# The last output tiles of a fused attention and gated-FFN kernel: column parts in PSUM tiles of their own, a narrow last part, and products left in PSUM

## The chip, the cores and the metric

One core of one Trainium2 chip. The metric is device time in microseconds (us) of one execution, lower is better. Every result is the median of several executions; all runs were fast (granted clock 0.998 to 1.000).

The engines are called by their names, with the profile's short forms: TensorE (PE; its weight loads PEld), VectorE (DVE), ScalarE (ACT), GpSimd (POOL), SyncE (SP). A "q" after a name is the engine's sequencer or queue. PSUM is the on-chip buffer that TensorE's results go to in this kernel, in tiles of 2 x 512 fp32 columns, of which each 512 are called a bank here; SBUF is the one that this kernel keeps the rest of its tiles in. A DMA's landing is its end in the profile.

## The reference, cut to what matters

```python
x  = A_x                                  # 1 x 2048 x 640
xn = layernorm(x)
s  = attention(xn)                        # 32 heads of 192, last 512 keys; ends in  o @ wo  (6144 x 640)
g  = silu(ffn(xn))                        # gated FFN
return x + s * g
```

The kernel treats the heads as 16 pairs and the 2048 rows as 4 blocks of 4 tiles of 128. Only the end is in question: for the last pair, each tile of 128 rows gets `o @ wo` for 640 columns (in PSUM), is multiplied by `g` (the tile `g2`), has the rest added (`sacc`, which already holds `x` and the other pairs' part times `g`), and is stored.

## The kernel before

The output tiles of the last pair. Tiles of block 2 and 3 take two groups of three matmuls per half, since they also take up the pair before.

```python
def wo_mm(ps, i, qt, n, first=True, end=True):
    for j in range(3):
        nc.tensor.matmul(ps, OTs[i][:, 3*qt+j, :], pairs[i//NB]["wo"][:, j, n*HD:(n+1)*HD], ...)   # HD = 320

def wo_last(b, qt, eng):
    i, t = last * NB + b, 4 * b + qt
    ob  = xrs[t] if b < 2 else finp.tile([P, D], bf, name="ob", bufs=4)
    s_f = finp.tile([P, 2, HD], f32, name="s_f", bufs=4)
    split = b == NB - 1 and qt == 3                       # the very last tile
    sc = None if split else mm_tile() if b >= 2 and qt % 2 == 0 else sc_tile()
    ps = [(mm_tile()[:, 0, :] if split else sc[:, n, :])[:, 0:HD] for n in range(2)]
    for n, cols in enumerate(halves):
        # ... matmuls of half n into ps[n]
        if split:
            nc.vector.tensor_tensor(s_f[:, n, :], ps[n], g2[:, t, cols], ALU.mult)
            nc.vector.tensor_tensor(ob[:, cols], s_f[:, n, :], sacc[:, t, cols], ALU.add)
            (nc.scalar if n else nc.sync).dma_start(...)
    if split:
        return
    nc.vector.tensor_tensor(s_f[:], sc[:, :, 0:HD], g2[:, t, :]..., ALU.mult)
    eng.tensor_tensor(ob[:], s_f[:]..., sacc[:, t, :], ALU.add)
    stores.append((t, ob))

# ... at the end
for b in (2, 3):
    for qt in range(4):
        store(0 if (b, qt) == (3, 3) else 3)
        wo_last(b, qt, V if b == 3 and qt % 2 == 0 else G)     # V = VectorE, G = GpSimd
```

`mm_tile()` and `sc_tile()` each hand out one of two PSUM tiles of two banks in turn: four tiles, eight banks. A product is always VectorE's (GpSimd reads only SBUF in this kernel), and the addition is GpSimd's, except for two tiles of block 3 and the last tile.

The softmax here doesn't subtract the row's maximum and nothing guards it: scores larger than these inputs give would overflow.

Of the kernel before, what the change touches and what calls it, by code (L numbers as in the profile page):

```python
# [10 lines left out]
ALU = mybir.AluOpType  # L11
# [4 lines left out]
def kernel(  # L16
# [13 lines left out]
    nc = tc.nc  # L30
    P = nc.NUM_PARTITIONS

    x2 = A_x.flatten_outer_dims()
    out2 = out.flatten_outer_dims()
    Sq, D = x2.shape
# [9 lines left out]
    NB = Sq // 512  # L45
# [5 lines left out]
    HD = D // 2  # L51
    scale = float(Dh) ** -0.5
    EPS = 1e-5
    bf = dt.bfloat16
    f32 = dt.float32
# [6 lines left out]
    kk, vv, wq, wo = A_k_cache[0], A_v_cache[0], A_wq, A_wo  # L62
# [8 lines left out]
    def sc_tile():  # L71
        return psum.tile([P, 2, 512], f32, name="sc", tag="sc")

    def mm_tile():
        return psum.tile([P, 2, 512], f32, name="mm", tag="mm")
# [5 lines left out]
    g2 = res.tile([P, T, D], bf, name="g2")  # L81
# [14 lines left out]
    pairs = {}  # L96
# [68 lines left out]
    with ExitStack() as fctx:  # L165
# [154 lines left out]
        first = {f: [sc[:, s, :] for s in range(2)] for f, sc in ((0, sc_tile()), (1, sc_tile()))}  # L320
# [89 lines left out]
    finp = ctx.enter_context(tc.tile_pool(name="fin", bufs=2))  # L410
    sacc = sapool.tile([P, T, D], f32, name="sacc")

    NS = NPAIR * NB
    turn_t = smpool.tile([P, 1], f32, name="turn_t", bufs=1)
    last = NPAIR - 1
    Ps, OTs, Obs, xrs = {}, {}, {}, {}
# [91 lines left out]
    def pv_full(i, q2):  # L508

        pr, b = divmod(i, NB)  # L510
        if q2 == 0:
            Obs[i] = opool.tile([P, 4, 2, Dh], bf, name="O_b")
            tag = "OT_l" if late(i) and pr < last else "OT_b"
            OTs[i] = otpool.tile([P, 12, P], bf, name=tag, tag=tag, bufs=2 if tag == "OT_l" else 3)
        O_b, OT_b = Obs[i], OTs[i]
        alone = i < 2 or (pr == last and 2 * b + q2 < 5)
        acc = sc_tile() if alone and b == 1 else mm_tile()
        for k in range(2):
            qt = 2 * q2 + k
            for h in range(2):  # L520
                for kc in range(KC):
                    nc.tensor.matmul(  # L522
                        acc[:, k, h * 256 : h * 256 + Dh + 1],
                        Ps[i][kc][:, h, qt * P : (qt + 1) * P], V_p[:, kc, h, 0 : Dh + 1],
                        start=(kc == 0), stop=(kc == KC - 1),
                    )
        divide(i, q2, acc, alone)
# [6 lines left out]
    def late(i):  # L534
        return i // NB >= NPAIR - 2 and i % NB >= 2

    def wo_mm(ps, i, qt, n, first=True, end=True):
        for j in range(3):
            nc.tensor.matmul(  # L539
                ps, OTs[i][:, 3 * qt + j, :], pairs[i // NB]["wo"][:, j, n * HD : (n + 1) * HD],  # L540
                start=(first and j == 0), stop=(end and j == 2),
            )

    def follows(m, earlier):
        tc.add_manual_dep(
            m.ins, earlier.ins.name,
            mybir.DependencyInfo(mybir.DependencyClass.Sync, mybir.DependencyReason.DATA),
            reason="row tiles change banks",
        )
# [48 lines left out]
    def wo_full(i, qt):  # L598
        pr, b = divmod(i, NB)
        t = 4 * b + qt  # L600
        sc = sc_tile()
        for n in range(2):
            wo_mm(sc[:, n, 0:HD], i, qt, n)
        s_t = sacc[:, t, :].rearrange("p (n d) -> p n d", n=2)
        if pr == 0:
            nc.vector.tensor_copy(out=s_t, in_=sc[:, :, 0:HD])
        else:
            nc.vector.tensor_tensor(s_t, s_t, sc[:, :, 0:HD], ALU.add)

        if pr == last - 1 or late(i + NB):  # L610
            nc.gpsimd.tensor_tensor(sacc[:, t, :], sacc[:, t, :], g2[:, t, :], ALU.mult)
            if pr < last - 1:
                add_x(t)

    def add_x(t):
        nc.gpsimd.tensor_tensor(sacc[:, t, :], sacc[:, t, :], xrs[t][:], ALU.add)

    stores = []

    def wo_last(b, qt, eng):  # L620
        i, t = last * NB + b, 4 * b + qt
        ob = xrs[t] if b < 2 else finp.tile([P, D], bf, name="ob", bufs=4)
        s_f = finp.tile([P, 2, HD], f32, name="s_f", bufs=4)
        halves = [slice(n * HD, (n + 1) * HD) for n in range(2)]
        split = b == NB - 1 and qt == 3
        sc = None if split else mm_tile() if b >= 2 and qt % 2 == 0 else sc_tile()
        ps = [(mm_tile()[:, 0, :] if split else sc[:, n, :])[:, 0:HD] for n in range(2)]
        for n, cols in enumerate(halves):
            if late(i):
                wo_mm(ps[n], i - NB, qt, n, end=False)  # L630
            wo_mm(ps[n], i, qt, n, first=not late(i))
            if split:
                nc.vector.tensor_tensor(s_f[:, n, :], ps[n], g2[:, t, cols], ALU.mult)
                nc.vector.tensor_tensor(ob[:, cols], s_f[:, n, :], sacc[:, t, cols], ALU.add)
                (nc.scalar if n else nc.sync).dma_start(
                    out=out2[t * P : (t + 1) * P, cols], in_=ob[:, cols]
                )
        if split:
            return
        nc.vector.tensor_tensor(  # L640
            s_f[:], sc[:, :, 0:HD], g2[:, t, :].rearrange("p (n d) -> p n d", n=2), ALU.mult
        )
        eng.tensor_tensor(ob[:], s_f[:].rearrange("p n d -> p (n d)"), sacc[:, t, :], ALU.add)
        stores.append((t, ob))

    def store(left):
        while len(stores) > left:
            t, ob = stores.pop(0)
            nc.sync.dma_start(out=out2[t * P : (t + 1) * P, :], in_=ob[:])
# [20 lines left out]
    for pr in range(NPAIR):  # L670
        for b in range(NB):
            i = pr * NB + b
# [22 lines left out]
        for b in range(NB):  # L695
            i = pr * NB + b
            if i < 2:
                two(pv(i, 0), pv(i, 1))
                if i == 0:
                    q_rows(*EARLY)  # L700
            elif pr < last - 1:
                woven(i)
            else:
                for q2 in range(2):
                    pv_full(i, q2)
                    wo_full(i - 2, 2 * q2)
                    wo_full(i - 2, 2 * q2 + 1)
            if b == 0 and pr + 2 < NPAIR:
                load_k(pr + 2)
            elif b == 1 and pr + 2 < NPAIR:  # L710
                load_wq(pr + 2)
            elif b == 2:
                load_wo(pr + 1)
    i = last * NB
    V, G = nc.vector, nc.gpsimd
# [3 lines left out]
    for b, q2, more in ((0, 0, (2, 1)), (0, 1, (3, 0)), (1, 0, (3, 1)), (1, 1, None)):  # L719
        for k in range(2):  # L720
            wo_last(b, 2 * q2 + k, G)
        if more:
            pv_full(i + more[0], more[1])
    for b in (2, 3):
        for qt in range(4):
            store(0 if (b, qt) == (3, 3) else 3)
            wo_last(b, qt, V if b == 3 and qt % 2 == 0 else G)


# [28 lines left out]
```

## Time and profile before

| | before |
|---|---|
| median of the first 3 runs | 925.28 us (924.81 to 925.31) |
| profiled span | 923.7 us |
| TensorE busy | 917.0 us |
| first matmul of block 2 of the last pair (the start of the "tail" in what follows) | 905.48 us |
| last issue of a store | 920.95 us, 15.47 after the tail's start |
| end of the span | 18.2 us after the tail's start |

How to read it: TensorE is busy from one end to the other (917.0 of 923.7 us), so almost all of the time is out of reach of this change. The prediction below shows the lines of the profile.

### The profile page before, as it was taken

The numbers are of one execution on the slowest core, as the hardware profiler recorded it, in microseconds if no ns is written. First come the engines' busy times: TensorE is split into PE (matmuls) and PEld (weight loads), VectorE is DVE, ScalarE is ACT, GpSimd is POOL, SyncE is SP. The second block draws the span as 40 slices with busy tenths as digits, with TensorE's granted clock in tenths as the row PEclk, the third lists the DMA queues.
The fourth block names the chain that finished last, engine by engine and source line by source line (L and its number), as shares of the span: only waits on it lengthen the run. The fifth ranks groups of instructions, "written<-read, shape, count | busy, mean of one in ns | idle before, by whom it ended". The sixth has DMA issues, their size and how long they took to land.

```text
span 923.7 us, 25785 instructions
## 1 busy us (share of the span) xinstructions
PE 917.0 (99%) x11101; PEld 626.2 (68%) x11101; DVE 576.2 (62%) x844; ACT 473.7 (51%) x847; POOL 100.1 (11%) x387
## 2 busy tenths in 40 slices
PE   9999999999999999999999999999999999999997
PEld 5455555575858585868686867676767777776665
DVE  6433331467676767676666667676767676767655
ACT  4222223546464656555556565655555555556561
POOL 0000000000000000000000000000000000002977
PEclk9999999999999999999999999999999999999999
DMA  9321510035544434444536252636271717162524
GB/s 294 77 53 35 114 35 1 1 71 95 83 82 83 83 79 87 74 91 68 98 59 106 60 107 53 112 51 115 44 121 41 126 37 129 36 132 74 135 57 140
DMA packets 243810, 77.18 MB, mean 84 GB/s; under 512 B 224624, under 2 KB 243696, under 8 KB 243696
## 3 DMA queue, kind: packets, MB, share of 16 engines
q1 hardware_dynamic: 242640, 74.72, 41.5%
q8 instruction: 87, 1.43, 0.7%
q10 hardware_dynamic: 1056, 0.82, 0.3%
q14 instruction: 27, 0.22, 0.1%
HBM read 39.45 MB, written 2.62 MB: 46 GB/s over the span
## 4 chain that ended last, share of the span: by engine, by line
PE 98%; DMA 1%; DVE 0%; ACTq 0%; issue 0%; DVEq 0%
PE mm L430 22%; PE sc L565 19%; PE sc L444 18%; PE mm L470 16%; PE sc L276 11%; PE mm L298 6%; PE sc L539 3%; PE mm L522 2%; PE mm L539 1%; DMA wu_sb<-in_B_w_up_dram 1%; PE mm L276 0%; PE mm L311 0%; PE sc L522 0%; PE sc L470 0%; PE mm L444 0%
## 5 line engine op out<-in xcount | busy, mean ns | idle before, releaser
L448 ACT ACTIVATE p_t<-sc 128x1024 bf16<-128x1024 f32 x254 | 252.9, 1022 | 128.6 <-PE sc L444 128.6
L435 DVE TENSOR_REDUCE qT<-mm 128x512 bf16<-128x1024 f32 x189 | 231.0, 1223 | 92.5 <-PE mm L430 90.0
L500 ACT ACTIVATE O_b<-mm,r 128x192 bf16<-128x192 f32 x486 | 164.6, 421 | 183.4 <-issue 159.2
L430 PE MATMUL mm<-xnT,wq_p 64*128 64x512 bf16 x1890 | 240.2, 377 | 0.0
L590 DVE TENSOR_TENSOR sacc<-sacc,sc 128x640 f32<-128x640 f32 x200 | 164.3, 821 | 89.5 <-PE sc L565 89.5
L565 PE MATMUL sc<-wo_p,OT_b 64*128 64x320 bf16 x2592 | 217.4, 296 | 0.0
L444 PE MATMUL sc<-qT,khat 64*128 64x512 bf16 x1524 | 198.4, 377 | 0.1
L470 PE MATMUL mm<-V_p,p_t 64*128 64x193 bf16 x3520 | 186.5, 243 | 0.0
L470 PEld LDWEIGHTS <-p_t 64*128 64x128 bf16 x3584 | 162.9, 93 | 12.3 <-issue 0.4
L430 PEld LDWEIGHTS <-wq_p 64*128 64x128 bf16 x1890 | 105.7, 94 | 94.5 <-issue 0.5
L565 PEld LDWEIGHTS <-OT_b 64*128 64x128 bf16 x2592 | 140.7, 94 | 21.1
L444 PEld LDWEIGHTS <-khat 64*128 64x128 bf16 x1536 | 85.9, 94 | 79.0 <-issue 0.4
L553 POOL MEMSET turn_t<- 128x1 f32 x328 | 32.2, 98 | 696.4 <-PE mm L470 474.0
L284 DVE TENSOR_TENSOR hT<-sc,sg 128x512 bf16<-128x512 f32 x46 | 31.7, 690 | 85.2 <-ACT sg L283 85.1
L283 ACT ACTIVATE sg<-sc 128x512 bf16<-128x512 f32 x46 | 27.3, 596 | 72.4 <-PE sc L276 72.4
L276 PE MATMUL sc<-xnT,wu_sb 128*128 128x512 bf16 (+1 forms) x260 | 59.1, 355 | 0.5 <-DMA wu_sb<-in_B_w_up_dram 0.5
L276 PE MATMUL sc<-xnT,wg_sb 128*128 128x512 bf16 (+1 forms) x260 | 59.2, 355 | 0.0
L298 PE MATMUL mm<-wd_sb,hT 128*128 128x320 bf16 x384 | 56.6, 300 | 0.0
L489 DVE RECIPROCAL r<-mm 128x4 f32<-128x4 f32 x124 | 22.6, 183 | 47.4 <-PE mm L470 35.9
L298 PEld LDWEIGHTS <-hT 128*128 128x128 bf16 x384 | 37.5, 98 | 18.9
L276 PEld LDWEIGHTS <-wu_sb 128*128 128x128 bf16 x285 | 26.3, 98 | 27.4 <-DMA wu_sb<-in_B_w_up_dram 0.7
L276 PEld LDWEIGHTS <-wg_sb 128*128 128x128 bf16 x285 | 26.4, 98 | 23.1
(68 smaller groups left out, 373.6 us busy)
## 6 DMA issues: line engine op xcount, KB each, us to landing
wo_p<-in_A_wo_dram SPq DMA_DIRECT2D x16, 480.0 KB, 4.3
K_p<-in_A_k_cache_dram SPq DMA_DIRECT2D x32, 192.0 KB, 3.1
V_p<-in_A_v_cache_dram SPq DMA_DIRECT2D x32, 192.0 KB, 3.0
wq_p<-in_A_wq_dram SPq DMA_DIRECT2D x64, 80.0 KB, 3.2
wq_p<-in_A_wq_dram SPq DMA_DIRECT2D x16, 160.0 KB, 3.5
x_r<-in_A_x_dram SPq DMA_DIRECT2D x16, 160.0 KB, 3.7
x_t<-in_A_x_dram SPq DMA_DIRECT2D x14, 160.0 KB, 3.1
OT_b<-O_b SPq DMA_TRANSPOSE x124, 2.8
```

The source lines that it names most:

```text
L276: nc.tensor.matmul(out, w_sb[:, c, f * P : (f + 1) * P], xnT[:, c, qc], start=(c == 0), stop=(c == NC - 1),)
L298: nc.tensor.matmul(dn[:, 0:HD], hTs[b][:, f, ti * P : (ti + 1) * P], wd_sb[:, f, cols], start=(f == 0), stop=(f == NF - 1),)
L430: nc.tensor.matmul(q_ps[:, h, :], pairs[pr]["wq"][r, c, j * P : (j + 1) * P], xnT[r, c, b * 512 : (b + 1) * 512], start=(c == 0), stop=(c ...
L435: nc.vector.reduce_sum(qTs[i][:, j, :], q_ps[:, :, :].rearrange("p h n -> p n h"), axis=AX.X)
L444: nc.tensor.matmul(sc[:, h, :], khat[r, j, ks], qT[r, j, :], start=(j == 0), stop=(j == 2))
L448: nc.scalar.activation(p_t[:, :, :], sc[:, :, :], ACT.Exp, scale=scale)
L470: m = nc.tensor.matmul(acc[:, k, h * 256 : h * 256 + Dh + 1], Ps[i][kc][r, h, qt * P : (qt + 1) * P], V_p[r, kc, h, 0 : Dh + 1], start=(p ...
L500: nc.scalar.activation(O_b[:, qt, h, :], a_k[:, h, 0:Dh], ACT.Copy, scale=r[:, k, h, :])
L539: nc.tensor.matmul(ps, OTs[i][:, 3 * qt + j, :], pairs[i // NB]["wo"][:, j, n * HD : (n + 1) * HD], start=(first and j == 0), stop=(end an ...
L553: st["turn"] = nc.gpsimd.memset(turn_t[:], 0.0)
L565: m = nc.tensor.matmul(ps[:, n, 0:HD], OTs[i][r, 3 * qt + j, :], pairs[i // NB]["wo"][r, j, n * HD : (n + 1) * HD], start=(turn == 0 and j ...
L590: nc.vector.tensor_tensor(s_t, s_t, sc[:, :, 0:HD], ALU.add)
```

## The change

The intent: let the last tiles leave TensorE in smaller pieces, so that VectorE and GpSimd start on a half while TensorE does the other; let GpSimd and VectorE share the last tile; and keep in PSUM a product that VectorE itself adds to, so that its addition has one input in PSUM and one in SBUF.

```diff
-    def wo_mm(ps, i, qt, n, first=True, end=True):
+    def wo_cols(ps, i, qt, cols, first=True, end=True):
 ...
+    def finish(ps, t, cols, ob, s_f, eng):
+        like = ...                                   # shapes two banks as one row
+        to = ps if eng is V else like(s_f[:, cols])
+        V.tensor_tensor(to, ps, like(g2[:, t, cols]), ALU.mult)
+        eng.tensor_tensor(like(ob[:, cols]), to, like(sacc[:, t, cols]), ALU.add)
 ...
+    def wo_parts(qt, parts):
+        ...
+        for n, (width, eng, queue) in enumerate(parts):
+            cols, c0 = slice(c0, c0 + width), c0 + width
+            ps = (sc_tile() if n else mm_tile())[:, 0, 0:width]
+            wo_cols(ps, i - NB, qt, cols, end=False)
+            wo_cols(ps, i, qt, cols, first=False)
+            finish(ps, t, cols, ob, s_f, eng)
+            if queue:
+                queue.dma_start(out=out2[t * P : (t + 1) * P, cols], in_=ob[:, cols])
+        if not queue:
+            stores.append((t, ob))
 ...
-    for b in (2, 3):
-        for qt in range(4):
-            store(0 if (b, qt) == (3, 3) else 3)
-            wo_last(b, qt, V if b == 3 and qt % 2 == 0 else G)
+    for qt in range(4):
+        store(3)
+        wo_last(2, qt, G if qt else V)
+    for qt, engs in enumerate(((G, V), (G, G), (V, G))):
+        store(2 - qt)
+        wo_parts(qt, [(HD, eng, None) for eng in engs])
+    store(0)
+    wo_parts(3, ((384, G, nc.sync), (D - 384, V, nc.scalar)))
```

(The cut parts: `wo_last` loses its split branch and calls `finish`.)

More of the change, by code (lines that the diff above doesn't have):

```diff
@@ L535, in late @@
         return i // NB >= NPAIR - 2 and i % NB >= 2
-    def wo_mm(ps, i, qt, n, first=True, end=True):
+    def wo_cols(ps, i, qt, cols, first=True, end=True):
         for j in range(3):
             nc.tensor.matmul(
-                ps, OTs[i][:, 3 * qt + j, :], pairs[i // NB]["wo"][:, j, n * HD : (n + 1) * HD],
+                ps, OTs[i][:, 3 * qt + j, :], pairs[i // NB]["wo"][:, j, cols],
                 start=(first and j == 0), stop=(end and j == 2),
             )
+    HALVES = [slice(n * HD, (n + 1) * HD) for n in range(2)]
     def follows(m, earlier):
@@ L602, in wo_full @@
         for n in range(2):
-            wo_mm(sc[:, n, 0:HD], i, qt, n)
+            wo_cols(sc[:, n, 0:HD], i, qt, HALVES[n])
         s_t = sacc[:, t, :].rearrange("p (n d) -> p n d", n=2)
@@ L618 @@
     stores = []
+    def finish(ps, t, cols, ob, s_f, eng):
+        like = (lambda a: a.rearrange("p (n d) -> p n d", n=2)) if len(ps.shape) == 3 else (lambda a: a)
+        to = ps if eng is V else like(s_f[:, cols])
+        V.tensor_tensor(to, ps, like(g2[:, t, cols]), ALU.mult)
+        eng.tensor_tensor(like(ob[:, cols]), to, like(sacc[:, t, cols]), ALU.add)
     def wo_last(b, qt, eng):
@@ L622, in wo_last @@
         ob = xrs[t] if b < 2 else finp.tile([P, D], bf, name="ob", bufs=4)
-        s_f = finp.tile([P, 2, HD], f32, name="s_f", bufs=4)
-        halves = [slice(n * HD, (n + 1) * HD) for n in range(2)]
-        split = b == NB - 1 and qt == 3
-        sc = None if split else mm_tile() if b >= 2 and qt % 2 == 0 else sc_tile()
-        ps = [(mm_tile()[:, 0, :] if split else sc[:, n, :])[:, 0:HD] for n in range(2)]
-        for n, cols in enumerate(halves):
-            if late(i):
-                wo_mm(ps[n], i - NB, qt, n, end=False)
-            wo_mm(ps[n], i, qt, n, first=not late(i))
-            if split:
-                nc.vector.tensor_tensor(s_f[:, n, :], ps[n], g2[:, t, cols], ALU.mult)
-                nc.vector.tensor_tensor(ob[:, cols], s_f[:, n, :], sacc[:, t, cols], ALU.add)
-                (nc.scalar if n else nc.sync).dma_start(
-                    out=out2[t * P : (t + 1) * P, cols], in_=ob[:, cols]
-                )
-        if split:
-            return
-        nc.vector.tensor_tensor(
-            s_f[:], sc[:, :, 0:HD], g2[:, t, :].rearrange("p (n d) -> p n d", n=2), ALU.mult
-        )
-        eng.tensor_tensor(ob[:], s_f[:].rearrange("p n d -> p (n d)"), sacc[:, t, :], ALU.add)
-        stores.append((t, ob))
+        s_f = finp.tile([P, D], f32, name="s_f", bufs=4)
+        sc = mm_tile() if b == 2 and qt % 2 == 0 else sc_tile()
+        for n, cols in enumerate(HALVES):
+            if late(i):
+                wo_cols(sc[:, n, 0:HD], i - NB, qt, cols, end=False)
+            wo_cols(sc[:, n, 0:HD], i, qt, cols, first=not late(i))
+        finish(sc[:, :, 0:HD], t, slice(0, D), ob, s_f, eng)
+        stores.append((t, ob))
+    def wo_parts(qt, parts):
+        i, t, c0 = NS - 1, 4 * (NB - 1) + qt, 0
+        ob = finp.tile([P, D], bf, name="ob", bufs=4)
+        s_f = finp.tile([P, D], f32, name="s_f", bufs=4)
+        for n, (width, eng, queue) in enumerate(parts):
[8 more added lines that the diff above has]
+            stores.append((t, ob))
     def store(left):
```

## The prediction

> **What bounds the kernel now.** I began with the busy times of the page and its chain that ended last.
>
> ```profile
> PE 917.0 (99%) x11101; PEld 626.2 (68%) x11101; DVE 576.2 (62%) x844; ACT 473.7 (51%) x847; POOL 100.1 (11%) x387
> PE 98%; DMA 1%; DVE 0%; ACTq 0%; issue 0%; DVEq 0%
> ```
>
> TensorE is busy for 917.0 of 923.7 us and makes 98% of the chain. The diff leaves every matmul of the first 905 us as it is (`wo_full` calls the same three matmuls under another name). What can move is the end: the chain names TensorE up to 917.07, so some 6.6 us after it belong to others. So I read the chain from 915 us on, and then the timelines of VectorE, GpSimd and TensorE there (columns: start in us, us, engine, line, operation, out<-in, count, and in brackets what it waited for).
>
> ```profile
> 915.42 1.64 PE mm L539 x12
> 917.07 0.03 issue
> ...
> 917.16 0.84 DVE s_f L640
> ...
> 918.16 0.83 issue
> 918.99 0.49 DVE s_f L633
> 919.48 0.02 issue
> 919.50 0.49 DVE ob L634
> 919.99 0.41 DVE s_f L633
> 920.40 0.02 issue
> 920.43 0.49 DVE ob L634
> ```
>
> ```profile
> 913.90 0.82 DVE L640 TENSOR_TENSOR s_f<-mm,g 128x640 f32<-128x640 f32 x1 [0.81 <-POOL ob L643]
> 914.76 1.27 DVE L643 TENSOR_TENSOR ob<-s_f,sacc 128x640 bf16<-128x640 f32 x1
> 915.95 0.81 DVE L640 TENSOR_TENSOR s_f<-sc,g 128x640 f32<-128x640 f32 x1
> 917.16 0.82 DVE L640 TENSOR_TENSOR s_f<-mm,g 128x640 f32<-128x640 f32 x1 [0.40 <-PE mm L539]
> 918.02 1.05 DVE L643 TENSOR_TENSOR ob<-s_f,sacc 128x640 bf16<-128x640 f32 x1
> ```
>
> ```profile
> 909.30 6.04 POOL L643 TENSOR_TENSOR ob<-s_f,sacc 128x640 bf16<-128x640 f32 x4
> 916.84 1.54 POOL L643 TENSOR_TENSOR ob<-s_f,sacc 128x640 bf16<-128x640 f32 x1 [1.50 <-DVE s_f L640]
> ```
>
> ```profile
> 918.04 0.57 PE L539 MATMUL mm<-wo_p,OT_l 128*128 128x320 bf16 x3 [0.17 <-DVE s_f L640]
> ```
>
> Three things are to be seen. First, from 917.16 to 920.92 VectorE works without a break: the product of the last tile but one (0.82), its addition (1.05), then product and addition of two halves. The chain's 0.83 us of "issue" at 918.16 is not idle: by the timeline VectorE is adding until 919.07. Second, VectorE's two additions of 640 columns took 1.27 and 1.05 us, though one of 320 took 0.49 with nothing beside it. GpSimd was adding until 915.34 (909.30 + 6.04) and until 918.38. 914.76 + 1.27 = 916.03 is 0.69 after the first of these ends, and 919.07 is 0.69 after the second: the same remainder both times, as if VectorE waited for GpSimd to end. Third, TensorE stood still before 918.04: without a wait its second half tile would have begun at 917.71, 0.41 after the group at 917.30. Its PSUM tile was the one whose product ended at 917.98. After the last addition comes the store from ScalarE's queue:
>
> ```profile
> L635 ACTq DMA_DIRECT2D out_dram<-ob x1: 367/367/367, 921.0 to 921.0; - x1
> DMA to landing us min/median/max: 1.6/1.6/1.6
> ```
>
> It is issued at 920.95, lands 1.6 us later and the span ends at 923.7: 2.75 us from issue to end that the change does not touch.
>
> [...] no VectorE arithmetic of this trace writes fp32 PSUM, so its duration is not shown. [...] GpSimd's additions here start every 1.51 us (6.04/4) at 640. [...]
>
> **The change part by part.** TensorE's work keeps its columns: 12 matmuls of 320 columns per tile take 1.63 us, a half tile 0.82. In the last tile the first part is six matmuls of 384 columns, by proportion 0.98 us, the last six of 256, 0.65 us. The loads of weights (98 ns) stay shorter than a 256-column matmul (109 ns). Products have begun 0.27 us after TensorE starts the next tile (907.11 and 907.38).
>
> *Tile 0 of block 2* is now summed by VectorE, at 908.2 to 909.05, beside GpSimd and with no lock as the product is in PSUM. The next product comes at 909.01 anyway: cost under 0.05 us. GpSimd, busy without a break until 915.34 before, loses 1.51 us of work there.
>
> *Tiles of block 3 in halves.* TensorE's tile starts before were 1.63 apart; from them the halves are ready at 913.08, 913.90, 914.71, 915.53, 916.35 and 917.16. VectorE needs 0.48 for a product (the 320-column product above), 0.49 for a sum. Walking through: product 913.08 to 913.56 (GpSimd adds); 913.90 to 914.90 with the sum; 914.90 to 915.38; 915.53 to 916.01; 916.35 to 917.35 with the sum; 917.28 to 917.76. VectorE is idle between them, so it is not the bound. GpSimd has finished block 2 at about 914.65[...].
>
> *PSUM.* Each half has its own tile, so one is taken again only four halves later. The tightest case is the last part, which starts at 917.87 on a tile whose product ended at 916.01. No wait is left, so TensorE's 0.33 us go.
>
> *The last tile.* First part: TensorE 916.89 to 917.87, product ready 918.14, product 0.55 to 918.69[...]. The SP store is issued near 919.76. Second part: TensorE ends its issue at 918.52, product 918.79 to 919.21, sum to 919.67, ScalarE's store near 919.70. The two paths now lie beside each other where they had been in a row.
>
> *Sum.* The last issue moves from 920.95 to 919.76: 1.19 us less. Against it I set 0.15 us for the two stores meeting: they were issued 0.93 us apart and now together, and the SP one has 96 KB for 80. Net some 1.04 us. I choose 1.0: 925.28 - 1.0 = 924.3. In other terms: 0.33 is TensorE's wait, about 0.22 the lock in the last addition, the rest is that GpSimd works beside VectorE and that VectorE's pieces are smaller.
>
> **The rivals.** *A: GpSimd becomes the end.* If its fixed cost is nearer 0.4 us, 384 columns take about 1.07 and 320 about 0.95; its queue before the last part still empties by 918.8. The end is 0.1 to 0.15 later: 924.4. Its 1.55 us records at 640 are the only ones of this form, so nothing speaks firmly against it. *B: the in-place path is slow, or locks all the same.* If a PSUM-to-PSUM operation took 0.1 us more, the last sum would end at 919.85, still beside GpSimd's path: 924.4. If the sum waited for GpSimd, as those of before did, it would end some 0.3 after 919.73: 924.6. Against it speak the 200 accumulations of 821 ns that read one PSUM and one SBUF input. *C: the stores eat it.* The 160 KB store of the last tile but one leaves near 918.7 and the two parts at 919.7, so 320 KB drain together. If the landing stretches from 1.6 to 2.1 us, half the gain goes: 924.7. For it speaks that the DMA engines are well used after 918; against it, that the 80 KB store issued at 920.02 landed in 1.6 us with the 160 KB one of 919.10 still moving. *D: nothing comes*, if the end depends on some fixed step after the last landing; but that step would move with the landing, so I give it little: 925.2.
>
> **Range and chances.** The rivals lie between 924.3 and 924.7, and a gain of all terms without the 0.15 for the stores gives 924.1. The three runs of before spread over 0.5 us. I take 923.6 to 924.9. A change of 2% would be 18.5 us, more than the whole tail touched here: 1% for faster, 1% for slower, 98% within.
>
> **What would show it right or wrong.** In the changed profile TensorE should have no wait in its last 16 us and end its issue near 918.5. VectorE's sums of 320 columns should read about 490 ns, those of 640 about 824, while GpSimd is busy. [...] The last two issues should lie within 0.15 us of each other near 919.75, the landings at 1.6 to 1.75 us, and the span end near 922.7. A sum on VectorE that ends 0.3 us or more behind a GpSimd one would show the lock; landings over 2 us the stores; a TensorE wait in block 3 a PSUM tile held too long. The prediction is wrong if the time is above 924.9, or below 923.6, which only a shift of code or memory before the tail could bring.

The sum came to 1.19 us less 0.15, rounded to 1.0, so 924.3 us, and it stands, but a term of it is cut: from the first part's product, at 918.69, to the SP store at 919.76, with GpSimd's addition ending at 919.73 between. That step was the author's estimate; the trace of before has GpSimd's additions at 640 columns only (1.51 us from start to start). VectorE's 0.55 and 0.42 us (384 and 256 columns) can be had from that trace: a line through its 0.492 us at 320 columns and 0.825 at 640 gives 0.56 and 0.43. The 109 ns of a matmul of 256 columns is an estimate by proportion from the 1.63 us of 12 of 320. Rival A's 1.07 and 0.95 us are what a fixed part of 0.4 us, which is assumed, and the measured 1.51 us at 640 columns give. The 0.15 us for the stores is the author's estimate. The DMA engines that rival C calls well used after 918 had a busy share of 0.26 from 918 to 920 and of 0.41 from 920 to 922.

"The lock" is the text's name for what it read from the trace: two additions of VectorE with both inputs in SBUF took 1.27 and 1.05 us and ended 0.69 us after GpSimd's, while the product at 917.16, with one input in PSUM, took 0.82 us though GpSimd was adding from 916.84 to 918.38. That an addition with its product in PSUM would go the same way was an estimate from those products.

## The result, and the profile after

| | before | after |
|---|---|---|
| median | 925.18 us (924.81 to 925.66, 6 runs) | 924.28 us (923.96 to 924.41, 6 runs) |
| profiled span | 923.7 us | 922.5 us |
| start of the tail | 905.48 | 905.33 |
| last issue of a store, after that start | 15.47 us | 14.31 us |
| end of the span, after that start | 18.2 us | 17.2 us |

The ratio is 0.999 (95% interval 0.9977 to 1.0003): the same within 2%, and by that interval not even told from 1. Ratios here are the mean time of one kernel's fast runs over that of the other's of the same rounds, so not quite the ratio of the medians. The medians differ by 0.90 us, and the six times of each do not overlap (the slowest after is 924.41, the fastest before 924.81). The span fell by 1.2 us; 0.15 of that lies before the tail, where the two kernels do the same, so it is run-to-run difference. The tail itself is 1.05 us shorter.

The busy times of the page and the chain that ended last, after:

```profile
PE 915.9 (99%) x11085; PEld 624.4 (68%) x11101; DVE 575.7 (62%) x847; ACT 473.7 (51%) x847; POOL 101.6 (11%) x390
PE 98%; DMA 1%; DVE 0%; ACTq 0%; issue 0%; POOLq 0%; POOL 0%; DVEq 0%
```

Nothing is to be seen at that scale, except that GpSimd has joined the chain. The end is seen in the timelines of VectorE, GpSimd, SyncE and ScalarE from 915.3 us on (columns as in the prediction):

```profile
915.31 0.49 DVE L626 TENSOR_TENSOR s_f<-sc,g 128x320 f32<-128x320 f32 x1 [0.21 <-PE sc L539]
916.12 0.50 DVE L626 TENSOR_TENSOR mm<-mm,g 128x320 f32<-128x320 f32 x1 [0.32 <-PE mm L539]
916.71 0.49 DVE L627 TENSOR_TENSOR ob<-mm,sacc 128x320 bf16<-128x320 f32 x1
917.12 0.48 DVE L626 TENSOR_TENSOR s_f<-sc,g 128x320 f32<-128x320 f32 x1
917.98 0.56 DVE L626 TENSOR_TENSOR s_f<-mm,g 128x384 f32<-128x384 f32 x1 [0.38 <-PE mm L539]
918.57 0.43 DVE L626 TENSOR_TENSOR sc<-sc,g 128x256 f32<-128x256 f32 x1
919.04 0.42 DVE L627 TENSOR_TENSOR ob<-sc,sacc 128x256 bf16<-128x256 f32 x1
```

```profile
917.74 1.88 POOL L627 TENSOR_TENSOR ob<-s_f,sacc 128x320 bf16<-128x320 f32 x2 [0.72 <-DVE s_f L626]
```

```profile
919.64 0.33 SPq L654 DMA_DIRECT2D out_dram<-ob  x1
```

```profile
919.49 0.40 ACTq L654 DMA_DIRECT2D out_dram<-ob  x1
```

VectorE now waits for TensorE between its pieces (0.21, 0.32, 0.38 us): the backlog of before is gone. Its additions of 320 and 256 columns take 0.49 and 0.42 us while GpSimd is adding beside them (the one at 916.71 for its first 0.30 us only, as GpSimd stops at 917.01). Those of before, 1.05 and 1.27 us, had 640 columns; one of that width with its product in PSUM stands in block 2, all of it inside one of GpSimd's:

```profile
908.08 0.82 DVE L627 TENSOR_TENSOR ob<-mm,sacc 128x640 bf16<-128x640 f32 x1
907.68 1.54 POOL L627 TENSOR_TENSOR x_r<-s_f,sacc 128x640 bf16<-128x640 f32 x1
```

At the end GpSimd's last addition, the 384 columns (0.99 us), ends at 919.61 and VectorE's last at 919.46, side by side. The two stores are issued 0.15 us apart. TensorE shows no wait any more in these 16 us.

### The profile page after: what moved, and what is told of

It reads as the page before. It is cut to its first block, busy times and chain, and to the rows that moved or that the text cites. A ratio compares the mean times of both kernels' runs of the same rounds, so it can differ in the third digit from the quotient of the medians.

```text
span 922.5 us, 25778 instructions
## 1 busy us (share of the span) xinstructions
PE 915.9 (99%) x11085; PEld 624.4 (68%) x11101; DVE 575.7 (62%) x847; ACT 473.7 (51%) x847; POOL 101.6 (11%) x390
## 3 DMA queue, kind: packets, MB, share of 16 engines
q8 instruction: 87, 1.43, 0.7%
## 4 chain that ended last, share of the span: by engine, by line
PE 98%; DMA 1%; DVE 0%; ACTq 0%; issue 0%; POOLq 0%; POOL 0%; DVEq 0%
PE mm L430 22%; PE sc L567 19%; PE sc L444 18%; PE mm L470 16%; PE sc L276 11%; PE mm L298 6%; PE sc L539 3%; PE mm L522 2%; PE mm L539 1%; DMA wu_sb<-in_B_w_up_dram 1%; PE mm L276 0%; PE mm L311 0%; PE sc L470 0%; PE sc L522 0%; PE mm L444 0%
```

## The experiments

Twelve runs (eleven kernels, as the changed one ran twice), each of five rounds, were made in three calls; each call was on one chip and shared nine runs of the kernel before (medians 925.14, 925.18 and 925.44). In every case the result was correct; the interval of the ratio leaves out 1 only for after_again (faster) and one_psum_tile (slower). Executions of one run scatter by 0.4 to 1.5 us, so the times tell apart little below 0.5 us. What decides is the tail in the trace, one trace for each edit: the time from its start to the last issue of a store, 15.47 us before and 14.31 after.

| run | edit | last issue after tail's start | median time | less that of before |
|---|---|---|---|---|
| after_again | the changed kernel | 14.31 | 923.99 | -1.15 |
| sbuf_sums | products VectorE sums go to SBUF | 15.00 | 924.71 | -0.43 |
| before_psum_sums | before, with PSUM sums alone | 15.58 | 925.50 | +0.36 |
| one_psum_tile | both parts in one PSUM tile | 18.12 | 927.86 | +2.72 |
| whole_tiles | block 3, tiles 0 to 2 whole | 15.05 | 924.65 | -0.53 |
| even_halves | last tile 320 and 320 | 14.30 | 924.16 | -1.02 |
| b2_on_gpsimd | block 2, tile 0 on GpSimd | 14.37 | 924.48 | -0.70 |
| after_third | the changed kernel | 14.32 | 924.37 | -0.81 |
| sbuf_sums_b2_gpsimd | both of these | 14.95 | 925.15 | -0.29 |
| last_on_vector | last tile on VectorE alone | 14.70 | 924.63 | -0.81 |
| before_last_shared | before, first half of last tile on GpSimd | 15.31 | 925.04 | -0.40 |
| parts_352 | last tile 352 and 288 | 14.73 | 924.46 | -0.98 |

**The anchors.** The changed kernel, unedited.

> The changed kernel once more, as the anchor for the others of this call. The measure is the tail: from the first matmul of block 2 of the last pair (the first on OT_l for an output tile, 905.33 us in the changed kernel's trace) to the end of the span (922.5), 17.2 us; in the kernel before it is 18.2 us (905.48 to 923.7). Expected: 17.2 us within 0.1, and a time 0.9 us (0.6 to 1.2) below the kernel before on the same chip. If the gain were only the luck of the first six runs, tail and time would come back near those of before.

> The changed kernel again, the anchor of this call. Tail 17.2 us within 0.1.

Both came as expected: tails of 17.1 and 17.2 us (spans 922.5 and 923.0, starts 905.36 and 905.84), times 1.15 and 0.81 us below before. The second trace ends 0.5 us later than the first, all of it from before the tail.

**Products in SBUF again.**

```diff
-        to = ps if eng is V else like(s_f[:, cols])
+        to = like(s_f[:, cols])
```

> The changed kernel with the one thing undone that products which VectorE itself sums stay in PSUM: they go to SBUF again, so each of those sums has two SBUF inputs. Theory (the sum waits until GpSimd's addition ends): the last sum of 256 columns takes about 0.87 us in place of 0.425, as it starts near 919.04 (on the changed kernel's clock), GpSimd adds until 919.61 and the remainder after GpSimd's end was 0.69 us at 640 columns, so about 0.29 at 256. ScalarE's store is then issued near 919.9 and the tail is 0.25 us longer (0.15 to 0.4). The sum in block 2 and the two halves in block 3 are stretched too, by 0.3 to 1 us, without moving the end. Rival (it is the smaller pieces and the sharing between engines that help, and where the product lies does not matter): every sum keeps 0.43, 0.49 and 0.82 us and the tail stays at 17.2.

VectorE's and GpSimd's timelines of this run, in part:

```profile
908.18 1.85 DVE L627 TENSOR_TENSOR ob<-s_f,sacc 128x640 bf16<-128x640 f32 x1
...
914.30 1.43 DVE L627 TENSOR_TENSOR ob<-s_f,sacc 128x320 bf16<-128x320 f32 x1
...
916.97 0.66 DVE L627 TENSOR_TENSOR ob<-s_f,sacc 128x320 bf16<-128x320 f32 x1
...
919.12 1.27 DVE L627 TENSOR_TENSOR ob<-s_f,sacc 128x256 bf16<-128x256 f32 x1
```

```profile
915.34 1.11 POOL L627 TENSOR_TENSOR ob<-s_f,sacc 128x320 bf16<-128x320 f32 x1
916.42 0.86 POOL L627 TENSOR_TENSOR ob<-s_f,sacc 128x320 bf16<-128x320 f32 x1
917.24 1.11 POOL L627 TENSOR_TENSOR ob<-s_f,sacc 128x320 bf16<-128x320 f32 x1
918.30 0.86 POOL L627 TENSOR_TENSOR ob<-s_f,sacc 128x320 bf16<-128x320 f32 x1
919.12 0.99 POOL L627 TENSOR_TENSOR ob<-s_f,sacc 128x384 bf16<-128x384 f32 x1
```

The rival is out: every one of the four sums is stretched, the same additions that took 0.82, 0.49, 0.49 and 0.42 us with the product in PSUM. The last ends at 920.39, 0.28 us after GpSimd's (919.12 + 0.99), as expected (0.29). But the last issue moved by 0.69 us, not by 0.25. What the expectation left out stands in the second fence: two of GpSimd's additions of 320 columns took 1.11 us for 0.86, and each lies at the end of a stretched VectorE sum. So the waiting goes both ways.

**Products in SBUF, and tile 0 of block 2 on GpSimd.** Both edits at once (the second is `wo_last(2, qt, G)`). My theory was that the one sum of 1.85 us in block 2, which held back the next product and left GpSimd idle for 1.50 us, was the surplus.

> VectorE's products in SBUF again (as in the run that did this alone, where the last issue of a store came 15.00 us after the tail's start against 14.31 in the changed kernel, 0.69 more and not the 0.25 expected), and tile 0 of block 2 on GpSimd besides, so VectorE has no sum in block 2. Theory: most of the surplus came from that one sum in block 2, which took 1.85 us for 0.82 because it waited for GpSimd, held back the next product and left GpSimd idle for 1.50 us in place of 0.55. Without it GpSimd runs on unbroken and ends near 14.35 after the start, the last sum waits for it and ends 0.27 later: last issue at 14.65 (14.55 to 14.75). Rival (the surplus comes from the stretched sums in block 3): about 15.0, as there.

Measured: 14.95. The theory fell, and the rival, the sums in block 3, holds. GpSimd ran without a break from 909.33, as I had wanted, and still ended 14.65 us after the start, not at 14.35; its five last additions were again of 1.11, 0.86, 1.11, 0.86 and 0.99 us. Two times 0.25 us of waiting, less the 0.20 us that GpSimd stood idle in block 3 of the run below with tile 0 on GpSimd, is the 0.3 us; the last sum's wait of 0.28 us behind it makes 0.58, which is 14.95 less the 14.37 of that run. This pair shows what the sums of block 3 cost where GpSimd has hardly any idle time left. It does not split the 0.69 us of the run before, where GpSimd had 1.5 us less to do but began a whole microsecond later (910.85, 5.43 after the start, for 4.43).

**PSUM sums alone, in the kernel before.**

```diff
+        to = sc[:, :, 0:HD] if eng is V else s_f[:]
-            s_f[:], sc[:, :, 0:HD], g2[:, t, :]..., ALU.mult
+        nc.vector.tensor_tensor(to, sc[:, :, 0:HD], like(g2[:, t, :]), ALU.mult)
# and the same for the halves of the last tile
```

> The kernel before with this part alone: the products that VectorE sums stay in PSUM; tiles, widths and engines as before. Theory: the lock goes, so the sum that took 1.05 us takes 0.83 and the one of 1.27 too, but the PSUM tile of the last tile but one is now held until that sum ends, 0.87 us longer, so TensorE's wait before its last half tile grows from 0.33 us to about 1.2 us. The last half is then ready at 919.99 on the clock of before, and its sum ends near 920.99 in place of 920.92. Tail 18.2 to 18.4 us: no gain, or a loss of 0.1. Rival (the lock was the loss and this part alone repairs it): 0.2 us or more off the tail, 18.0 or less.

TensorE's wait in this run, and VectorE's first whole tile with what GpSimd did beside it:

```profile
918.50 0.58 PE L539 MATMUL mm<-wo_p,OT_l 128*128 128x320 bf16 x3 [1.10 <-DVE ob L643]
```

```profile
914.35 0.82 DVE L643 TENSOR_TENSOR ob<-mm,sacc 128x640 bf16<-128x640 f32 x1
913.35 1.57 POOL L643 TENSOR_TENSOR ob<-s_f,sacc 128x640 bf16<-128x640 f32 x1
```

The lock (VectorE's wait for GpSimd) is gone: this sum takes 0.82 us for 1.27, though GpSimd adds until 914.92. (The last whole tile's sum, at 917.62, takes 0.82 for 1.05, but only 0.16 us of it lies beside GpSimd's, so it tests little.) And nothing is won: the PSUM tile is held through the addition, and TensorE's last half starts 13.49 us after the tail's start for 12.56. Last issue 15.58, 0.11 later than before, as expected. By itself this part trades a wait of VectorE for one of TensorE.

**Both parts in one PSUM tile.**

```diff
+        both = sc_tile() if qt % 2 else mm_tile()
         for n, (width, eng, queue) in enumerate(parts):
-            ps = (sc_tile() if n else mm_tile())[:, 0, 0:width]
+            ps = both[:, n, 0:width]
```

> The changed kernel with both parts of a tile of block 3 in the two banks of one PSUM tile, not in two tiles of their own; widths and engines as in the changed kernel. Theory 1 (the halves are what counts; own tiles only if waits go by whole tiles): a product of a first part waits for its own matmuls alone, starts as before, and the tail stays 17.2 us. Theory 2 (waits go by the whole tile, so own tiles are needed): each first part's product waits for the second part's matmuls too, 0.8 us in tiles 0 to 2 and 0.65 us in the last, so GpSimd's last sum ends near 920.2 and the tail is 0.6 us longer, 17.8.

```profile
913.43 0.57 PE L539 MATMUL mm<-wo_p,OT_l 128*128 128x320 bf16 x3 [0.65 <-DVE s_f L626]
915.92 0.57 PE L539 MATMUL sc<-wo_p,OT_l 128*128 128x320 bf16 x3 [0.70 <-DVE s_f L626]
918.95 0.57 PE L539 MATMUL mm<-wo_p,OT_l 128*128 128x320 bf16 x3 [1.24 <-DVE ob L627]
921.62 0.49 PE L539 MATMUL sc<-wo_p,OT_l 128*128 128x256 bf16 x3 [0.72 <-DVE s_f L626]
```

Both theories missed. The waits do go by the whole tile, but the other way round from what I had written: the product of a first part does not wait for the second part's matmuls, the second part's matmuls wait until VectorE is done with the first part (its product, and in tile 2 its sum as well), though they write to another bank. That is the order in which the kernel's code has them. TensorE and VectorE take turns. The last part's first matmul comes 16.34 us after the tail's start for 12.38, and the kernel is 2.7 us slower than the one before. Without tiles of their own, parts cost far more than they bring.

**Block 3's tiles 0 to 2 whole.**

```diff
-    for qt, engs in enumerate(((G, V), (G, G), (V, G))):
-        store(2 - qt)
-        wo_parts(qt, [(HD, eng, None) for eng in engs])
+    for qt, eng in enumerate((V, G, V)):
+        store(2 - qt)
+        wo_last(3, qt, eng)
```

> The changed kernel with tiles 0 to 2 of block 3 whole again (one product of 640 columns each; VectorE, GpSimd, VectorE sum them, VectorE's in PSUM); the last tile stays in parts of 384 and 256. Theory (a backlog on VectorE): the product of tile 2 begins only when all its matmuls are done, at 917.01 on the changed kernel's clock, and with its sum holds VectorE to 918.7, so the last tile's first product starts there and not at 917.98, GpSimd ends near 920.3 and the tail is 0.68 us longer (0.5 to 0.8): 17.85. Rival (only the last tile's cut matters): tail 17.2 to 17.3.

Measured: 15.05, so 0.74 us later (expected 0.68). The last tile's first product starts 13.35 us after the tail's start for 12.65. Halving the three tiles before the last is worth more than what was tried on the last tile alone (0.39 and less). The edit also gives VectorE two whole sums of the three tiles where it had two halves, which no run separates; with tile 2's sum on GpSimd instead, its 1.54 us and the 0.99 of the last tile in a row would end at about 919.9, 15.1 after the start, by an estimate from this trace's durations, so the end would hardly be earlier. TensorE has no wait here either; its last part begins 12.39 us after the start, as in the changed kernel (12.38). The span's tail grew by 0.5 us (17.7), as the store landed faster here, in 1.6 us for 1.8.

**The last tile in even halves.** `(HD, G, ...), (HD, V, ...)` for `(384, G, ...), (D - 384, V, ...)`.

> The changed kernel with the last tile in two parts of 320 instead of 384 and 256. Theory: GpSimd's path gets shorter (0.86 for 0.99 us, end near 919.46) and VectorE's longer (product 0.49, sum 0.49: end near 919.66 for 919.46), so the later of the two issues moves from 919.64 to about 919.7: tail 17.2, at most 0.1 us longer. Rival (the narrow last part is what makes the gain): tail 17.4 or more.

Measured: 14.30 for 14.31. The narrow last part is worth nothing that shows: what it takes from VectorE's path (sum ends 14.26 after the start for 14.13) it gives to GpSimd's (14.08 for 14.28).

**Tile 0 of block 2 on GpSimd.** `wo_last(2, qt, G)` for `wo_last(2, qt, G if qt else V)`.

> The changed kernel with tile 0 of block 2 summed by GpSimd again. GpSimd then has 1.5 us more to do, against 1.27 us that it stood idle in the changed kernel's tail, and its queue should run without a break into the last part: end near 919.7 for 919.61. Theory: tail 0.1 us longer (0 to 0.2). Rival A (the tile matters because GpSimd was the bound of the whole tail): 0.3 us or more. Rival B (VectorE was burdened for nothing): tail shorter than 17.2.

Measured: 14.37, 0.06 later, as expected. GpSimd's 1.5 us more fill what had been its idle time (0.55 and 0.72 us in the changed kernel, 0.20 left here).

**The last tile on VectorE alone.** `(384, V, ...)` for `(384, G, ...)`.

> The changed kernel with both parts of the last tile summed by VectorE (products in PSUM). Theory: VectorE does product, sum, product, sum one after the other from 12.65 us after the tail's start: 0.56 + 0.56 + 0.43 + 0.43 and steps, last issue at 14.64, 0.33 later than in the changed kernel. Rival (GpSimd, with 0.99 us for a sum that VectorE does in 0.56, is the slower choice): last issue at 14.3 or earlier.

Measured: 14.70, 0.39 later (expected 0.33).

**GpSimd's share alone, in the kernel before.**

```diff
-                nc.vector.tensor_tensor(ob[:, cols], s_f[:, n, :], sacc[:, t, cols], ALU.add)
+                (V if n else G).tensor_tensor(ob[:, cols], s_f[:, n, :], sacc[:, t, cols], ALU.add)
```

> The kernel before with one edit: GpSimd sums the first half of the last tile, VectorE the second, both from SBUF as before. Theory: VectorE's sum waits for GpSimd's (from 919.55 to 920.41 on the clock of before) and ends about 0.36 after it, so the last issue comes 15.3 us after the tail's start for 15.47: a gain of 0.15 us only. TensorE's wait before the last half stays 0.33. Rival (sharing the last tile is the gain, wherever the product lies): VectorE's sum ends 0.49 after its product and the last issue, now GpSimd's, comes at 15.0.

```profile
919.51 0.85 DVE L634 TENSOR_TENSOR ob<-s_f,sacc 128x320 bf16<-128x320 f32 x1
```

```profile
919.15 0.86 POOL L634 TENSOR_TENSOR ob<-s_f,sacc 128x320 bf16<-128x320 f32 x1 [1.16 <-DVE s_f L633]
```

Measured: 15.31, a gain of 0.16 (expected 0.15). VectorE's sum of 320 columns took 0.85 us in place of 0.49 and ended 0.35 after GpSimd's.

**352 and 288 columns.** An attempt to beat both, by balancing the two last paths.

> The changed kernel with the last tile in 352 and 288 columns, between the 384 and 256 of the changed kernel (SP's store last, at 14.31 after the tail's start) and the even halves (ScalarE's last, at 14.30). By the durations seen, GpSimd's path ends near 14.2 and VectorE's too: last issue at 14.2 to 14.25, a gain of under 0.1 us, which the times will hardly show. If it is not earlier than 14.28, something other than the two paths sets the end.

The trace shows another 0.5 us instead, in VectorE's timeline:

```profile
917.06 0.49 DVE L627 TENSOR_TENSOR ob<-mm,sacc 128x320 bf16<-128x320 f32 x1 [0.64 <-DMA out_dram<-ob]
```

The tile `ob` has four buffers, and tile 2 of block 3 takes the one of tile 2 of block 2 again. That tile's store was issued at 912.75 and took 4.2 us to land, which ends at 916.95. In the three traces of the changed kernel the same store took 3.4, 2.0 and 3.6 us, and no sum waits for it. The time (0.98 us below before) is like that of the changed kernel. Whether the width brings the 0.1 us is left open, and so is why one store takes 2 to 4 us to land. No run was left for a fifth buffer of `ob`, which is what I would try next.

## Why the prediction was right

**The total.** 924.3 predicted, 924.28 measured, inside 923.6 to 924.9. The tail shows that the gain was no accident of the median: 1.05 us shorter where the working had 1.04. That the totals agree to 0.02 us is luck: the median of before moved to 925.18 with three more runs, so the medians differ by 0.90, and on two other chips by 1.15 and 0.81.

**The last issue.** Predicted 1.19 us earlier, measured 1.16 (15.47 less 14.31). Against the stores' meeting the prediction had set 0.15 us; from last issue to end it took 2.86 us for 2.75, so 0.11. The landings were 1.7 and 1.8 us, where 1.6 to 1.75 had been named, so one lies just above, but none over 2: rival C did not come.

**Durations.** VectorE's estimates held. Products of 384 and 256 columns: 0.56 and 0.43 us (0.55 and 0.42 in the walk of the last tile). GpSimd on 320 and 384 columns: records of 0.86 and 0.99 us. The in-place product: 0.50 us for 320 columns, against 0.49 into SBUF, so rival B's slow PSUM path is 0.01 us and not 0.1.

**No lock with the product in PSUM.** Right, and shown by the run with products in SBUF: the same sums with the product in SBUF took 0.66 to 1.85 us. With it in PSUM they took 0.42 to 0.82 us. What was shown is these sums.

**No wait of TensorE.** Right: none in block 3 by the trace, and with one PSUM tile for two parts there are four.

**The split of the gain.** Here the prediction was wrong, though its total was right. Its last lines of the sum gave 0.33 us to TensorE's wait and 0.22 to the lock, as if these were shares. By the traces TensorE's wait alone cost the kernel before nothing: with PSUM sums the last product starts 1.03 us after its first matmul (919.53 less 918.50), so in the kernel before it could have begun near 919.07 (an estimate from that), while VectorE, busy without a break since 917.16, came to it at 919.91. In the kernel before, taking away the lock alone brought -0.11 us and sharing the last tile alone 0.16. Undone singly in the changed kernel, the product in PSUM is worth 0.69, the halves of tiles 0 to 2 are worth 0.74, GpSimd in the last tile 0.39, PSUM tiles of their own for the parts 3.81: more than the 1.16 in all. So what a part is worth depends on the others. What is shown: the product in PSUM lets both engines add at once, and the halves bring VectorE to the last tile 0.70 us sooner (12.65 for 13.35). It is not the halves that end TensorE's wait: with whole tiles there is none either. There, as in the changed kernel, the last part's matmuls write a tile of `sc_tile()`, in the kernel before the one of `mm_tile()` that tile 2 had held. Changing that alone was not run. Two parts of the change are worth next to nothing: the 256 columns (-0.01 us) and tile 0 of block 2 on VectorE (0.06, from one trace).

**What was mis-seen along the way.** Not in the prediction but in the expectations: that a lock between two engines costs only the one that waits first (0.25 expected, 0.69 measured), and which side waits when two parts share a PSUM tile (TensorE, four times, 0.65 to 1.24 us).

## What to carry to other kernels

At the end of a kernel where one engine has been busy all along (TensorE 99%, before and after here), what is left is the last pieces' way through the other engines: read it from timelines by hand, engine by engine, since the shares of busy time do not show it. Cut the last tiles so that the next engine can begin early, but give every piece a buffer of its own, as a wait may be for the whole buffer (here the last issue came 3.81 us later with shared ones); and when VectorE and GpSimd add at once, try VectorE with one operand in PSUM (here 0.49 us for 320 columns, for 0.66 and 1.43 with both in SBUF). Try such parts together: here two of them alone brought -0.11 and 0.16 us, because each only moved the wait.

## What the traces show of durations and waits

- How much of a VectorE sum with both operands in SBUF is still to run when GpSimd's addition ends: 0.69 us of 0.82 (640 columns, the kernel before), 0.34 to 0.35 of 0.49 (320, sbuf_sums and before_last_shared), 0.28 of 0.42 (256, sbuf_sums), so 0.13 to 0.15 us of it passes during the wait. On GpSimd's side: with 0.39 us of VectorE's sum still to run, its 0.86 us became 1.11 (sbuf_sums, twice).
- A product from PSUM into the same place took 0.83, 0.50 and 0.43 us at 640, 320 and 256 columns in the changed kernel, at 640 and 320 columns 0.01 us more than into SBUF (0.82 and 0.49).
- With the two parts of a tile in one PSUM tile of two banks, the waits went by the whole tile, and over four tiles that cost 3.81 us (one_psum_tile).
- An fp32 addition of GpSimd with bf16 output took 0.86, 0.99 and 1.54 us at 320, 384 and 640 columns in the changed kernel.
- The landing of a 160 KB store among other stores took from 1.8 us (the last two of the kernel before) to 4.2 us (parts_352) in these tails.
